# Gated mix of a recurrent memory attention and a GeGLU layer: one transpose excursion for k and q, o and v pieces in turn, fills in other gaps, scratch laid out anew

## The chip, the core and the metric

The kernel runs on one core of one Trainium2 chip. The metric is the device time of one execution in microseconds, as the median of several runs. TensorE (PE), VectorE (DVE), ScalarE (ACT), GpSimd (POOL) and SyncE (SP) run their own instruction streams in order and wait for each other on semaphores. Weights and activations are bf16, sums are held in PSUM as fp32.

## The reference, cut to what matters

```python
def A(x, mem0, Wq, Wk, Wv, Wo):            # x 1 x 2048 x 1024, 32 heads of 128, segments of 32 rows, memory of 8
    mem = mem0
    for s in range(64):
        h = concatenate([mem, x[:, 32*s:32*s+32]], axis=1)         # 40 rows
        q, k, v = (einsum('btd,dhe->bhte', h, W) for W in (Wq, Wk, Wv))
        scores = where(mask, einsum('bhqe,bhke->bhqk', q, k) * 128 ** -0.5, -1e9)
        o = einsum('bhqk,bhke->bhqe', softmax(scores), v)
        o = einsum('bhte,hed->btd', o, Wo)
        mem, out[s] = o[:, :8], o[:, 8:]
    return concatenate(out, axis=1)

def B(x, w_gate, w_up, w_down):            # 1024 x 3584, 1024 x 3584, 3584 x 1024
    return gelu(x @ w_gate) * (x @ w_up) @ w_down

g = sigmoid((x * gate_w).sum(-1, keepdims=True))
out = g * A(x) + (1 - g) * B(x)
```

A is a recurrence: each of its 64 steps needs the 8 memory rows that the step before left. The four weight matrices of A have 8 MB each, 32 MB together, and do not fit in SBUF; every step needs all of them.

## The kernel before

Three stages follow each other. A first stage transposes x, computes the gate and four of the 28 column blocks of the feed-forward layer, and fills SBUF with weights. Then come the 64 steps of the recurrence. Then the rest of the feed-forward layer and the mix.

**Steps and weights.** A step walks 64 positions in a fixed order (`walk`, line 327). A position is one piece of 512 KB of Wk, Wq, Wv or Wo: 128 rows by 16 heads, or two heads of Wo. `(m, r, i)` names piece `i` of matrix `m` in half `r` of the step; the half with `r = 0` works on 16 heads, `r = 1` on the other 16, and the next step begins with the half that was last. The walk is k and q of half 0 in turn, v of half 0, k and q of half 1, o of half 0, v of half 1, o of half 1. SBUF holds 52 pieces; 12 slots are shared by a pair of pieces, one of each half (`PAIRS`, line 318). When a shared slot's piece was used in half 0 (`spent`, line 385), SP fetches the other one (`fetch`, line 371, issue at line 378), so that 12 fetches of 512 KB are issued in a step. `proj` (line 784) computes a position: four matmuls in four 32-column tiles of TensorE (lines 796 and 779; 807 for o).

**Rows.** A segment's 32 rows and 8 memory rows make 40. The tile `hT` (line 525) has the transposed 24 first rows of the segment and the 8 memory rows. The last 8 rows (the rest) depend on no memory: for four segments at a time their q, k, v are computed ahead of the steps that need them, with the pieces that are in SBUF anyway. These are the fills (`fill`, line 822, eight positions each). Their results go to the scratch tensors `qk_scr` and `v_scr` in DRAM and come back one step ahead of use as `qkr` (line 534) and `vB` (line 538). Their attention outputs go to `o_scr`, come back as `oR`, and are multiplied with Wo by `wo` (line 837, also eight positions).

**One half of a step.** ScalarE evacuates k and q from PSUM into `tok` and `tok2` (line 677). TensorE turns each in an excursion to four 128 x 128 transposes (line 690); VectorE copies the results to `kT` and `qT` (line 680). `rest_k` (line 888, on POOL) adds the rest's k. `scores` (lines 711 to 718) does scores and softmax: a chain through VectorE and ScalarE, ten operations, whose results are `tA` (line 734) and `tB` (line 741). `attend` (line 752) needs `tA` and `vA`, `attend_tail` (line 762) `tB` and `vB`. ScalarE and VectorE evacuate the result to `oT`, and POOL copies the rest's part to `oRc` (line 773).

**Order.** `on(m, r, n, ...)` puts work ahead of position `n` of a part of the walk. In front of o of half 0 stand the eight positions of the first fill (`f1`), put between the evacuations, the two transposes, attend and its tail; `scores` of half 1 stands one position later. In front of o of half 1 stand the eight positions of the second fill (`f2`), six of them ahead of attend. At the step's end (from line 1018) ScalarE copies the output to `a_bf`, TensorE turns it in two transposes (line 1025), VectorE writes the 8 memory columns of the next `hT` (line 1027), and the next step starts. The output's store, `a_scr` from `a_bf` (line 1035), is issued from POOL within the next step. `pA`, which softmax writes, shares memory with `a_bf`.

The dependence tracker `_Prog` adds the semaphore waits. PSUM is tracked by bank, SBUF by 64-byte cells, and a DMA that has its own lane waits until the lane's last one has landed.

Of the kernel before, what the change touches and what calls it, by code (L numbers as in the profile page):

```python
# [195 lines left out]
def bass_gated_mix__memory_aug_recurrent_mem_tr__geglu_ffn__prompt_kernel(  # L196
# [20 lines left out]
    NR = 24  # L217
# [14 lines left out]
    with ExitStack() as es:  # L232
# [12 lines left out]
        v_scr = nc.dram_tensor("v_scr", [NSEG, NB, 16, 2, 128], BF16)  # L245
# [45 lines left out]
        qT = al("qT", [128, 4, 4, 32])  # L291
        cur[0] += 128
# [6 lines left out]
        vA = al("vA", [128, 4, 128], at=oT.off)  # L299
        tok2 = al("tok2", [128, 512], at=oT.off + 1024)  # L300
        tA = al("tA", [128, 8, 32], at=qT.off)
        tB = al("tB", [128, 8, 32], at=qT.off + 512)
        E8 = al("E8", [128, 8, LQ], at=qT.off + 512)
# [10 lines left out]
        oR2 = al("oR2", [128, RB, 16], at=odd0 + 1024)  # L314
        NSLOT = NLOW + (top - cur[0]) // PIECE


        PAIRS = {"k": (0, 2), "q": (0,), "v": (0, 1, 2, 3, 4, 6), "o": (0, 2, 4)}
# [8 lines left out]
        walk = both(0) + one("v", 0) + both(1) + one("o", 0) + one("v", 1) + one("o", 1)  # L327
# [112 lines left out]
        st0 = [al(f"st0{i}", [128, 512], at=slots[-1].off + 1024 * i) for i in range(4)]  # L440
        st1 = [stage] + [al(f"st1{i}", [128, 512], at=odd0 + 1024 * i) for i in range(2)]
# [81 lines left out]
        def load_h(s):  # L523
            t = hTs[s % 2]
            op("pool", lambda e: e.dma_start(t[:, :, :].rearrange("p k c -> p (k c)"), xq_scr[s // 4, :, s % 4, :]),
               rd=[("D", "xq", s // 4)], wr=[t.r()], lane=f"h{s % 2}")
# [5 lines left out]
        def load_qk(s, r):  # L532
            u = r ^ (s % 2)
            op("pool", lambda e: e.dma_start(qkr[:, r, :, :], qk_scr[:, s, 2 * u:2 * u + 2, :]),
               rd=[("D", "qk", s // 4, 2 * u), ("D", "qk", s // 4, 2 * u + 1)], wr=[qkr.r(256 * r, 256 * r + 256)], lane=f"qkr{r}")

        def load_v(s, us=slice(0, 2)):
            op("pool", lambda e: e.dma_start(vB[:, us, :].rearrange("p u c -> p (u c)"),
                                             v_scr[s][:, :, us, :].rearrange("i h u c -> h i (u c)")),
               rd=[("D", "v", s // 4, g, u) for g in range(4) for u in range(us.start, us.stop)], wr=[vB.r()], lane="vb")  # L540
# [13 lines left out]
        inits = [k for k in [at_step(p, 0) for p in range(24)] + [(m, 1, i) for m in "kqv" for i in range(8)]  # L554
# [129 lines left out]
        def evac(bank, t):  # L684
            act_copy(t[:, :], PB[bank][:, :], [BK(bank)], [t.r()])

        def trans4(e, t=tok, head=False):
            for j in range(4):
                to = PBV[TT][:, 0:512].rearrange("p (g j y) -> p j g y", g=4, j=4)[:, j] if head else PBV[TT][:, j * 128:(j + 1) * 128]
                ins = e.transpose(to, t[:, j * 128:(j + 1) * 128], ident[:, :])  # L690
            return ins

        def trans_pe(t):
            op("pe", lambda e: trans4(e, t), rd=[t.r(), ident.r()], wr=[BK(TT)])

        def trans(to, t):
            if t:
                trans_pe(t)
            i_ap = PBV[TT][:, 0:512].rearrange("p (j g c) -> p (j g) c", g=4, c=32)
            dve_copy(to[:, :, :, 0:32].rearrange("p j g c -> p (j g) c"), i_ap, [BK(TT)], [to.r()])  # L700
# [5 lines left out]
        def scores(r, mid=None):  # L706

            def f(e):
# [8 lines left out]
                for g in range(4):  # L717
                    ins = e.matmul(PB[SS][32 * g:32 * g + 32, 0:320].rearrange("p (a c) -> p a c", a=4)[:, :, LQ:80],
                                   lhsT=qkr[:, r, 0, 32 * g:32 * g + 32], rhs=kT[:, :, g, :],
                                   start=False, stop=True, skip_group_check=True)  # L720
                return ins
            op("pe", f, rd=[qT.r(), kT.r(), ident.r(), mS.r(), qkr.r(256 * r, 256 * r + 128)], wr=[BK(SS)])
            op("pool", lambda e: e.memset(pB[:, :].bitcast(FP32), 0.0), wr=[pB.r()])
            op("dve", lambda e: e.tensor_reduce(nm, sS, AX.X, ALU.max, negate=True), rd=[BK(SS)], wr=[st8.r(0, 8)])
            op("dve", lambda e: e.tensor_tensor(out=sS, in0=sS, in1=b8(nm, LQ), op=ALU.add), rd=[BK(SS), st8.r(0, 8)], wr=[BK(SS)])  # L725
            op("act", lambda e: e.activation(E8[:, :, :].rearrange("p a c -> p (a c)"), PB[SS][:, 0:320], ACTF.Exp, scale=scale),  # L726
               rd=[BK(SS)], wr=[E8.r()])
            if mid:
                mid()
# [14 lines left out]
        bo = (B0, B1, B2, SS)  # L744

        def attend(u):
# [11 lines left out]
        def attend_tail(u):  # L758
# [9 lines left out]
            for g in range(4):  # L768
                cp[("act", "dve")[g % 2]](oT[:, g, :, :].rearrange("p j c -> p (j c)"), PB[bo[g]][:, 0:n], [BK(bo[g])],
                                          [oT.r(g * n, (g + 1) * n)])  # L770
# [5 lines left out]
        bank_of = {("k", 0): B0, ("q", 0): B1, ("v", 0): B2, ("k", 1): B0, ("q", 1): F2, ("v", 1): B0}  # L776
# [36 lines left out]

        def fill(m, u, b, h=hR):
            ks = [(m, u, i) for i in range(8) if i not in PAIRS[m]] + [(m, u, i) for i in PAIRS[m]]
            out = []
            for n, k in enumerate(ks):
# [7 lines left out]
                out.append(lambda f=f, w=w: op("pe", f, rd=[h.r(), w.r()], wr=[BK(b)]))  # L825
            return out

        def wo(u, b, t=oR, ends=(True, True), at_end=False):
            out = []
            for i in range(8):  # L830
                w = (xo.get(("o", u, i)) if at_end else None) or slots[home["o", u, i]]

                def f(e, i=i, w=w):
                    for hh in range(2):
                        for g in range(4):
                            c = hh * 1024 + g * 256
                            ins = e.matmul(PB[b][32 * g:32 * g + 32, 0:256], lhsT=t[:, :, 2 * i + hh], rhs=w[:, c:c + 256],  # L837
                                           start=(ends[0] and i == 0 and hh == 0), stop=(ends[1] and i == 7 and hh == 1))
                    return ins
                out.append(lambda f=f, w=w: op("pe", f, rd=[t.r(), w.r()], wr=[BK(b)]))  # L840
# [8 lines left out]
        def fill_evac(m, u, b, st):  # L849
            t = st if m == "v" else tok  # L850
            act_copy(t[:, :], PB[b][:, :], [BK(b)], [t.r()])

        def fill_trans(m):
            op("pe", lambda e: trans4(e, tok, m == "q"), rd=[tok.r(), ident.r()], wr=[BK(TT)])

        def fill_put(st, how):
            cp[how](st[:, :].rearrange("p (i x c) -> p x i c", i=4, x=16), PBV[TT][:, 0:512].rearrange("p (x i c) -> p x i c", x=16, i=4),
                    [BK(TT)], [st.r()])

        def fill_store(m, u, G, st):  # L860
            if m == "v":
                for g in range(4):
                    op("pool", lambda e, g=g: e.dma_start(  # L863
                        v_scr[4 * G:4 * G + 4, :, 4 * g:4 * g + 4, u, :].rearrange("s i j c -> (s i) j c"),
                        st[32 * g:32 * g + 32, :].rearrange("p (j c) -> p j c", j=4)), rd=[st.r()], wr=[("D", "v", G, g, u)], lane=f"fv{g}")
            else:
                m4 = 2 * u + (0 if m == "q" else 1)
                op("pool", lambda e: e.dma_start(qk_scr[:, 4 * G:4 * G + 4, m4, :], st[:, :].rearrange("p (i y) -> p i y", i=4)),
                   rd=[st.r()], wr=[("D", "qk", G, m4)], lane="fq")

        def mm0(m, u, b, t, G=0, h=hR):
# [3 lines left out]
            if m == "v":  # L875
                fill_store(m, u, G, t)

        def tr0(m, u, t, b, G=0):
            op("pe", lambda e: trans4(e, t, m == "q"), rd=[t.r(), ident.r()], wr=[BK(TT)])
            fill_put(b, "dve")  # L880
            if G == 0:
                x = 256 * u + 128 * (m == "k")
# [297 lines left out]
```

## Time and profile before

| | us |
|---|---|
| median of 10 runs | 2207.38 |
| lowest, highest | 2202.39, 2215.53 |
| the profiled execution's own time | 2202.52 |
| its span, first to last instruction | 2200.8 |
| TensorE busy in it | 2031.7 |
| VectorE, ScalarE, POOL busy in it | 931.3, 606.8, 623.6 |

The granted TensorE clock was 0.993 over the span. In the profile, an instruction stands under the line of the kernel that made it, which for helpers is the helper's line, and under the names of its tiles (`out<-in`). "PEld" is the loading of weights into TensorE's array. A wait is put down to the instruction whose end released it; "issue" is time in which an engine waited for nothing that the profile shows.

### The profile page before, as it was taken

Reading aid. Unit: us, or ns where it says so; the run is one execution under the profiler, and the core shown is the slowest. Engines: PE = TensorE matmul, PEld = TensorE weight load, DVE = VectorE, ACT = ScalarE, POOL = GpSimd, SP = SyncE. Lnnn points to the kernel's source line nnn. Section 1 sums busy time; section 2 is a strip of 40 time slices with the busy share of each in tenths; the row PEclk is TensorE's granted clock in tenths of the full one; section 3 lists DMA queues with packets and bytes.
Section 4 is the critical chain, followed back from the end, with each engine's and each line's share of the span. In section 5 each row is a group of like instructions: output and inputs, shape, how many; then the busy total and the mean of one; then the engine's idle time right before and its main releaser. Section 6 shows DMA issues by size and latency. Waiting matters only on the chain.

```text
span 2200.8 us, 76740 instructions
## 1 busy us (share of the span) xinstructions
PE 2031.7 (92%) x37842; PEld 930.1 (42%) x32178; DVE 931.3 (42%) x2154; ACT 606.8 (28%) x1296; POOL 623.6 (28%) x1155
## 2 busy tenths in 40 slices
PE   7779999999999998999999999999888999999999
PEld 4334444444444444444444444444344424243343
DVE  6433443344344343433443444344344526254362
ACT  4322222323223232222323232232222303132130
POOL 7224334332433433343333334333321000000000
PEclk9989999999999999999999999999999999999999
DMA  9978888888888788878888888888789400001000
GB/s 365 374 275 273 296 309 278 297 305 290 275 300 314 272 296 285 299 272 275 319 281 280 302 304 285 284 313 295 266 310 369 146 21 29 30 29 30 23 27 20
DMA packets 202660, 528.84 MB, mean 240 GB/s; under 512 B 29592, under 2 KB 46616, under 8 KB 202336
## 3 DMA queue, kind: packets, MB, share of 16 engines
q1 hardware_dynamic: 171760, 466.69, 59.6%
q0 software_dynamic: 30432, 56.99, 8.3%
q8 instruction: 274, 4.49, 0.8%
q14 instruction: 50, 0.41, 0.1%
q10 hardware_dynamic: 144, 0.26, 0.0%
HBM read 490.16 MB, written 33.55 MB: 238 GB/s over the span
## 4 chain that ended last, share of the span: by engine, by line
PE 60%; DMA 25%; DVE 5%; POOL 5%; issue 3%; SPq 1%; ACT 1%; POOLq 0%; DVEq 0%
PE pb L462 15%; PE pb L796 12%; DMA sl<-in_A_Wv_dram 8%; PE pb L779 8%; PE pb L807 7%; DMA sl<-in_A_Wk_dram 6%; PE pb L822 5%; DMA a_scr<-a_bf 5%; PE pb L1135 4%; DMA sl<-in_A_Wo_dram 3%; PE pb L690 3%; DVE oT L680 2%; DMA xr_scr<-xr 2%; POOL v_scr L863 1%; PE pb L837 1%
## 5 line engine op out<-in xcount | busy, mean ns | idle before, releaser
L796 PE MATMUL pb<-sl,hT 128*32 128x512 bf16 x8192 | 667.8, 381 | 46.9 <-issue 22.5
L779 PE MATMUL pb<-sl,hT 128*32 128x512 bf16 x4096 | 398.5, 379 | 0.0
L796 PEld LDWEIGHTS pb<-sl,hT 128*32 128x32 bf16 x8192 | 211.7, 96 | 435.7 <-issue 272.6
L807 PE MATMUL pb<-sl,oT 128*32 128x256 bf16 x8192 | 276.9, 277 | 18.1 <-issue 9.9
L773 POOL COPY oRc<-oT 128x128 bf16<-128x128 bf16 x128 | 95.7, 748 | 646.0 <-DVE oT L680 646.0
L677 ACT ACTIVATE tok<-pb 128x512 bf16<-128x512 f32 x318 | 176.4, 596 | 345.8 <-PE pb L796 320.6
L807 PEld LDWEIGHTS pb<-sl,oT 128*32 128x32 bf16 x8192 | 202.6, 97 | 80.3 <-ACT oT L677 45.2
L822 PE MATMUL pb<-sl,hR 128*32 128x512 bf16 x3072 | 210.4, 385 | 0.0
L680 DVE COPY kT<-pb 128x512 bf16<-128x512 bf16 x128 | 53.2, 415 | 317.3 <-PE pb L690 296.0
L462 PE MATMUL pb<-xT,wg 128*128 128x512 bf16 x768 | 181.5, 379 | 3.9 <-DMA wg<-in_B_w_gate_dram 3.9
L462 PE MATMUL pb<-xT,wu 128*128 128x512 bf16 x768 | 181.4, 379 | 0.8 <-DMA wu<-in_B_w_up_dram 0.8
L680 DVE CAST oT<-pb 128x256 bf16<-128x256 f32 x256 | 96.7, 419 | 181.9 <-PE pb L762 181.9
L690 PE MATMUL pb<-ident,tok 128*128 128x128 bf16 x1272 | 126.7, 222 | 41.3 <-DVE kT L680 34.8
L1135 PE MATMUL pb<-wd,GT 128*32 128x512 bf16 x1568 | 152.2, 379 | 0.0
L779 PE MATMUL pb<-wd,GT 128*32 128x512 bf16 x1568 | 152.2, 379 | 0.0
L677 ACT ACTIVATE vA<-pb 128x512 bf16<-128x512 f32 x128 | 76.4, 597 | 269.3 <-PE pb L796 269.3
L450 ACT ACTIVATE s<-pb 128x512 f32<-128x512 f32 x112 | 66.9, 597 | 289.3 <-PE pb L462 289.3
L690 PEld LDWEIGHTS pb<-ident,tok 128*128 128x128 bf16 x1272 | 72.0, 98 | 150.9 <-DVE kT L680 83.1
L677 ACT ACTIVATE oT<-pb 128x256 bf16<-128x256 f32 x256 | 84.3, 381 | 183.6 <-PE pb L762 183.6
L451 DVE SCALAR_TENSOR_TENSOR tp<-s,pb 128x512 f32<-128x512 f32 x112 | 76.7, 685 | 123.4 <-ACT s L450 123.0
L726 ACT ACTIVATE E<-pb 128x320 bf16<-128x320 f32 x128 | 56.0, 437 | 219.3 <-DVE pb L725 219.3
L462 PEld LDWEIGHTS pb<-xT,wg 128*128 128x128 bf16 x768 | 74.8, 98 | 95.7 <-issue 6.3
(104 smaller groups left out, 2226.0 us busy)
## 6 DMA issues: line engine op xcount, KB each, us to landing
sl<-in_A_Wv_dram SPq DMA_DIRECT2D x394, 512.0 KB, 9.4
sl<-in_A_Wo_dram SPq DMA_DIRECT2D x205, 512.0 KB, 5.9
sl<-in_A_Wk_dram SPq DMA_DIRECT2D x142, 512.0 KB, 7.4
sl<-in_A_Wq_dram SPq DMA_DIRECT2D x79, 512.0 KB, 6.8
qkr<-qk_scr POOLq DMA_DIRECT2D x126, 64.0 KB, 2.4
qk_scr<-stg POOLq DMA_DIRECT2D x59, 128.0 KB, 6.9
wd<-in_B_w_down_dram SPq DMA_DIRECT2D x7, 1024.0 KB, 15.0
xq_scr<-xTp SPq DMA_DIRECT2D x4, 1024.0 KB, 17.1
```

The lines of the kernel that those rows point to most:

```text
L450: op("act", lambda e: e.activation(s1[:, :], hg, ACTF.Square, scale=SQ), rd=[BK(bg)], wr=[s1.r()])
L451: op("dve", lambda e: e.scalar_tensor_tensor(out=t[:, :], in0=s1[:, :], scalar=1.0, in1=hg, op0=ALU.add, op1=ALU.mult), rd=[BK(bg), s1.r() ...
L462: ins = e.matmul(PB[bk][:, 0:FB], lhsT=w[:, kc, cc:cc + 128], rhs=x[:, :, :, kc, :].rearrange("p t i c -> p (t i) c"), start=(kc == 0), st ...
L677: op("act", lambda e: e.activation(o, i, ACTF.Copy), rd=rd, wr=wr)
L680: op("dve", lambda e: e.tensor_copy(o, i), rd=rd, wr=wr)
L690: ins = e.transpose(to, t[:, j * 128:(j + 1) * 128], ident[:, :])
L773: op("pool", lambda e: e.tensor_copy(oRc[:, u, :, :].rearrange("p c (g j) -> p g j c", g=4), diag), rd=[oT.r()], wr=[oRc.r(128 * u, 128 * ...
L779: return e.add_instruction(mybir.InstMatmult(name=nc.get_next_instruction_name(), start_tensor_calc=start, stop_tensor_calc=stop, tile_siz ...
L796: ins = again(e, g, *at, one, end) if k[0] == "q" else e.matmul(*at, start=one, stop=end)
L807: ins = e.matmul(PB[XO][32 * g:32 * g + 32, 0:256], lhsT=oT[:, gp_, 2 * jj + hh, 0:32], rhs=w[:, c:c + 256], start=(r == 0 and one and hh ...
L822: ins = e.matmul(PB[b][32 * g:32 * g + 32, :], lhsT=h[:, k[2], :], rhs=w[:, g * 512:(g + 1) * 512], start=(n == 0), stop=(n == 7))
L1135: ins = again(e, q, *a, j == 0, j == NJ - 1) if hf else e.matmul(*a, start=(j == 0), stop=(j == NJ - 1))
```

## The change

- k and q of a half are evacuated by ScalarE and VectorE side by side, and turned in one excursion of eight transposes (`trans8`, `turn`); ScalarE copies kT and VectorE qT.
- o of half 0 and v of half 1 alternate in the walk. v has 5 shared slots instead of 6, o 4 instead of 3.
- Fills: of the first fill (`fa`) two positions stand ahead of the first attend, one behind its tail, five ahead of the second attend. Of the second (`fb`), four stand behind the second attend's tail, two ahead of the step end's transposes and two behind them. `wo` is part of `fb`. Q and K of a fill are turned together in the next step and stored in one DMA.
- `scores` of half 0 stands at position 1 of k half 1 (before: 2), that of half 1 at position 3 of o half 0 (before: 1).
- vA of half 1 is evacuated in halves, one by ScalarE and one by VectorE.
- At the step's end one `a_bf` half is copied by VectorE, and the two transposes become eight small matmuls in 32-column tiles.
- `v_scr` is laid out with the 16 heads of a half together: one store of 1 KB runs instead of four, and two loads of 256 B runs instead of one of 512 B. `qk_scr` is stored with k and q together.
- `qkr`, `hT` and `vB` are loaded from SP's ring instead of POOL's. `a_scr`'s store is issued at the first position of the next step.

```diff
-        v_scr = nc.dram_tensor("v_scr", [NSEG, NB, 16, 2, 128], BF16)
+        v_scr = nc.dram_tensor("v_scr", [NSEG, NB, 2, 16, 128], BF16)
...
-        vA = al("vA", [128, 4, 128], at=oT.off)
+        vAs = [al("vA0", [128, 4, 128], at=oT.off), al("vA1", [128, 4, 128], at=tok.off)]
+        qT = al("qT", [128, 4, 4, 32], at=stage.off)
...
-        PAIRS = {"k": (0, 2), "q": (0,), "v": (0, 1, 2, 3, 4, 6), "o": (0, 2, 4)}
+        PAIRS = {"k": (0, 2), "q": (0,), "v": (0, 1, 2, 3, 4), "o": (0, 1, 2, 3)}
...
-        walk = both(0) + one("v", 0) + both(1) + one("o", 0) + one("v", 1) + one("o", 1)
+        walk = both(0) + one("v", 0) + both(1) + [x for y in zip(one("o", 0), one("v", 1)) for x in y] + one("o", 1)
...
+        def load_qk(s):
+            op("sp", lambda e: e.dma_start(qkr[:, :, :, :].rearrange("p u m c -> p (u m c)"), qk_scr[:, s].rearrange("p m c -> p (m c)")),
+               rd=[("D", "qk", s // 4, u) for u in range(2)], wr=[qkr.r()], lane="qkr")
+
+        def load_v(s, us=(0, 1), eng="sp"):
+            for u in us:
+                op(eng, lambda e, u=u: e.dma_start(vB[:, u, :], v_scr[s][:, u].rearrange("i h c -> h i c")),
+                   rd=[("D", "v", s // 4, u)], wr=[vB.r(128 * u, 128 * u + 128)], lane=f"vb{eng}{u}")
...
+        def trans8(ka, qa, head=False):
+            def f(e):
+                trans4(e, ka)
+                return trans4(e, qa, head, 512)
+            op("pe", f, rd=[ka.r(), qa.r(), ident.r()], wr=[BK(TT)])
...
-        bo = (B0, B1, B2, SS)
+        bos = ((XO, SS, B2, F2), (B0, B1, B2, SS))
...
             on("v", 0, 0, lambda: evac(bank_of["k", 0], tok))
-            on("v", 0, 0, lambda: evac(bank_of["q", 0], tok2))
-            on("v", 0, 4, lambda: trans(kT, tok))
-            on("v", 0, 7, lambda: trans(qT, tok2))
-            on("k", 1, 0, lambda: evac(bank_of["v", 0], vA))
-            on("k", 1, 2, lambda: scores(0))
+            on("v", 0, 0, lambda: evac(bank_of["q", 0], stage, "dve"))
+
+            def turn():
+                trans8(tok, stage)
+                heads(kT, "act", 0)
+                heads(qT, "dve", 512)
+            on("v", 0, 4, turn)
+            on("k", 1, 0, lambda: evac(bank_of["v", 0], vAs[0]))
+            on("k", 1, 1, lambda: scores(ua))
+            on("k", 1, 1, softmax)
...
             on("o", 0, 0, lambda: evac(bank_of["k", 1], tok))
-            on("o", 0, 0, lambda: evac(bank_of["q", 1], tok2))
-            on("o", 0, 0, some(f1, 4))
-            on("o", 0, 0, lambda: trans(kT, tok))
-            on("o", 0, 0, some(f1, 2))
-            on("o", 0, 0, lambda: trans_pe(tok2))
-            on("o", 0, 0, lambda: attend(ua))
-            on("o", 0, 0, lambda: attend_tail(ua))
-            on("o", 0, 0, lambda: trans(qT, None))
-            on("o", 0, 0, some(f1))
...
+            on("o", 0, 0, lambda: evac(bank_of["q", 1], stage, "dve"))
+            on("o", 0, 0, some(fa, 2))
+            on("o", 0, 0, lambda: attend(ua, 0))
+            on("o", 0, 0, lambda: attend_tail(ua, 0))
+            on("o", 0, 0, some(fa, 1))
+            on("o", 0, 0, turn)
+            on("o", 0, 3, lambda: scores(ub))
+            on("o", 0, 3, softmax)
+
+            def halves(bank, t):
+                evac(bank, t, "act", 0, 256)
+                evac(bank, t, "dve", 256, 512)
+            on("o", 1, 0, lambda: halves(bank_of["v", 1], vAs[1]))
+            on("o", 1, 0, some(fa))
+            on("o", 1, 0, lambda: attend(ub, 1))
+            on("o", 1, 0, lambda: attend_tail(ub, 1))
+            if k2 and k2[0] == "v":
+                on("o", 1, 0, lambda: evac(F1, tok))
+                on("o", 1, 0, lambda: store_v(k2[1], G, tok))
+            on("o", 1, 0, some(fb, 4))
             if not last:
-                on("o", 1, 0, lambda: load_qk(s + 1, 0))
-                on("o", 1, 0, lambda: load_qk(s + 1, 1))
-                on("o", 1, 0, lambda: load_v(s + 1))
+                on("o", 1, 0, lambda: load_qk(s + 1))
                 if s + 2 < NSEG:
                     on("o", 1, 0, lambda: load_h(s + 2))
+                on("o", 1, 0, lambda: load_v(s + 1))
...
-            for t in range(2):
+            for t, eng in enumerate(("act", "dve")):
                 cs = slice(128 * t, 128 * t + 128)
-                act_copy(a_bf[:, cs], PB[XO][:, cs], [BK(XO)], [a_bf.r(cs.start, cs.stop)])
...
+                cp[eng](a_bf[:, cs], PB[XO][:, cs], [BK(XO)], [a_bf.r(cs.start, cs.stop)])
+            run(fb, 2)
             if not last:
...
+                for t, bk, eng in ((0, B2, "dve"), (1, SS, "act")):
+                    def f(e, t=t, bk=bk):
+                        for g in range(4):
+                            c = 128 * t + 32 * g
+                            ins = e.matmul(PB[bk][32 * g:32 * g + 32, 0:32], lhsT=a_bf[:, c:c + 32],
+                                           rhs=ident[:, :].rearrange("p (g c) -> p g c", g=4)[:, :, NR:32], start=True, stop=True)
+                        return ins
...
+            run(fb)
+
+            def a_store(s=s):
...
+            pend = [(0, [a_store])]
+            if k1:
+                pend.append((0, [lambda: evac(F1, tok2), lambda: evac(F2, tok, "dve")]))
+
+                def fills_in(u=k1[1], G=G):
+                    trans8(tok2, tok, True)
+                    fill_put(fqk[:, :, 1, :], fqk.r(), "act")
+                    fill_put(fqk[:, :, 0, :], fqk.r(), "dve", 512)
+                    store_qk(u, G, fqk)
+                pend.append((3, [fills_in]))
```

## The prediction

> **What bounds the kernel now.** I read the page first, then busy time by stretch, the order of time of TensorE and of VectorE through one step, the waits, and the DMA issues.
>
> ```profile
> 0.00:122.00 122.00, 92.15 (x752) 44.20 (x724) 61.46 (x94) 42.15 (x76) 54.54 (x65) 0.94 1.00 373
> 122.00:1661.00 1539.00, 1409.50 (x32158) 677.39 (x28086) 628.94 (x1707) 446.51 (x1028) 548.40 (x1054) 0.99 0.84 291
> 1661.00:2200.00 539.00, 530.06 (x4940) 208.47 (x3372) 240.89 (x354) 118.17 (x193) 20.70 (x37) 1.00 0.19 67
> ...
> 1041.00:1059.00 18.00, 16.88 (x400) 8.26 (x344) 8.78 (x23) 4.90 (x10) 6.84 (x14) 1.00 1.01 353
> 1059.00:1064.50 5.50, 5.01 (x129) 2.53 (x112) 1.10 (x4) 1.59 (x5) 3.91 (x8) 1.00 0.41 120
> ```
>
> Columns: stretch, length, busy PE, PEld, DVE, ACT, POOL, clock, DMA share, GB/s. The 64 steps of the recurrence take 1539 of 2200.8 us; 62 intervals between their ends (hT copies, L1027) run from 144.5 to 1637.5, 24.08 us each. The feed-forward stage hardly meets the diff. In a step DMA is full for 18 us (1.01) and nearly idle for 5.5: two chains of almost equal length, the engines' and the weight stream's.
>
> ```profile
> 1018.97 1.04 PE L796 MATMUL pb<-sl,hT 128*32 128x512 bf16 x16
> 1019.93 0.40 PE L690 MATMUL pb<-ident,tok 128*128 128x128 bf16 x4
> 1020.26 0.83 PE L796 MATMUL pb<-sl,hT 128*32 128x512 bf16 x12
> ...
> 1028.43 0.40 PE L807 MATMUL pb<-sl,oT 128*32 128x256 bf16 x8
> 1029.13 0.32 PE L711 MATMUL pb<-mS,ident 128*32 128x320 bf16 x4 [0.30 <-DVE qT L680]
> ...
> 1036.43 1.93 PE L807 MATMUL pb<-sl,oT 128*32 128x256 bf16 x64
> 1038.74 0.40 PE L1025 MATMUL pb<-ident,a_bf 128*128 128x128 bf16 x2 [0.38 <-ACT a_bf L677]
> 1039.24 0.40 PE L796 MATMUL pb<-sl,hT 128*32 128x512 bf16 x4
> ```
>
> ```profile
> 1029.67 0.49 DVE L724 TENSOR_REDUCE st<-pb 128x8 f32<-128x320 f32 x1 [0.59 <-PE pb L718]
> 1032.42 0.45 DVE L734 STREAM_TRANSPOSE tA<-pA 128x256 bf16<-128x256 bf16 x1
> 1033.01 0.45 DVE L741 STREAM_TRANSPOSE tB<-pB 128x256 bf16<-128x256 bf16 x1
> ```
>
> The first fence is TensorE in order of time (start, length, what, count, and in brackets idle time before it and what ended it), the second VectorE in the same step. Four things to read. A position of four matmuls costs 0.216 us (16 matmuls, 0.86), one of Wo about the same. An excursion to four 128x128 transposes costs 0.43: 0.10 late, then 0.33. From the last Wo matmul's turn (1038.11) to the next step's first (1039.24), 1.13 us hold no projection. And the softmax chain: call its first scores matmul S (1029.13); tA is done at S+3.74, tB at S+4.33.
>
> ```profile
> DVE pA L732 <- DMA a_scr<-a_bf: 27.7, 27, 2.8
> PE pb L690 <- DVE kT L680: 34.8, 30, 11.1
> DVE kT L680 <- POOL kT L888: 20.6, 2, 15.7
> POOL qk_scr L868 <- DMA qk_scr<-st: 16.4, 3, 6.8
> ```
>
> ```profile
> sl<-in_A_Wv_dram SPq DMA_DIRECT2D x394, 512.0 KB, 9.4
> sl<-in_A_Wo_dram SPq DMA_DIRECT2D x205, 512.0 KB, 5.9
> qkr<-qk_scr POOLq DMA_DIRECT2D x126, 64.0 KB, 2.4
> ```
>
> The waits (total us, times, longest), then the DMA issues (times, KB each, median us from issue to landing). pA shares memory with a_bf, so softmax waits until a_bf is stored; that store is issued on POOL behind the V stores.
>
> **Part by part, us per step, plus is gained.**
> - Step end: two fills' positions (0.44) now run behind the last Wo, then the transposes, two more behind them. a_bf is ready 0.62 after 1038.11 (matmul 0.25, ACT 0.28 and two hops), so 0.18 is waited, 0.15 spent on the eight small matmuls that replace two transposes (bounds: 0.10, in which sixteen 40-column L715 start, and 0.24, the two transposes' own); the hT copy (0.175) hides under the second pair. Visible 0.33 of 1.13: +0.80. Fills themselves are moved, not added. Without that cover, 0.
> - k and q in one excursion: 0.10 + 0.33 + 4 x 0.06 = 0.67 for 0.86, twice: +0.39. The fills' excursion at the third position of the next step costs 0.67 in 28 of 64 steps, where before K's 0.43 was paid and Q's hid at step end: -0.10.
> - The wait of scores on qT (1028.65 to 1029.13) goes: six positions now lie between: +0.48.
> - The store of a_bf is first on POOL at the next step's start, past the V stores (2.2 us of issues), which become one. Gaps before L690 that hang on this sum to 26 us: +0.41. What is late next there is tB.
> - First attend: scores to attend was 5.1 us of PE work, now 0.31 + 14 x 0.216 + 2 x 0.216 = 3.76. tA just comes, the tail waits for tB: 4.37 against 3.99. Then stage: its cast on DVE is queued behind tB and takes 0.62 (two 256-column casts, 0.38 and 0.38, less one start of 0.15, since hT's 32 columns take 0.175), so the transposes wait 0.14 more: -0.52. Behind this on PE stands the alternating block, behind stage on DVE two oT copies and qT; qT is ready at S+6.2, scores come at S+6.9, so nothing more is late. Bounds: -0.38 if PE arrives later, -0.6 with 0.69 for the cast (as a 512-column tensor op).
> - Second attend: before, 4.7 us lay between; now five o and five v positions, five fills: 0.31 + 2.16 + 1.08 + 0.10 = 3.65. vA is now half DVE's, queued behind tB: 4.33 + 0.38 + 0.04 = 4.75. All of attend waits, and behind it on PE the Q or Wo fills and the second half of Wo: -1.10. Bounds: -0.6 (a PE stall falls inside the window) and -1.5 (slower hops).
> - Weights: 12 fetches as before (k 2, q 1, v 5 for 6, o 4 for 3). In the step from 1039.24 they landed at 4.9, 7.5, 9.4; 10.8, 12.9, 14.2, 15.5, 16.8, 18.0; 19.5, 20.8, 22.3. PE waits between matmul starts on weights sum to 31.5 us (k 15.7, v 11.6, o 4.2), to "issue" 38.7. One V fewer ahead and the small loads out of the way bring the last V to about 16.2; its use is at 16.0 to 16.5, and up to 1.1 of lateness falls into the second attend's wait: +0.18. K: half its waits, +0.12. The last o lands near 21.5, wanted at 20.6 to 21.4: -0.2 to -0.5, -0.25 taken. Issue stalls inside the two attends' windows are absorbed: 0.3 of 0.6, of that half, +0.07. Together +0.12; bounds -0.5 and +0.4.
> - Small loads on SP's ring: qkr, hT, vB (256 KB) stand behind the four o fetches. They wait only for PE work that precedes the next fetch in program order, so no fetch is held (vB's load waits for the second attend's tail, and behind it on SP stand the next step's K fetches, due 4 us later); they land about 23, qkr is wanted 2.6 into the next step. POOL loses four issues (0.55 each). Taken 0, bounds -0.2 and +0.1.
> - tok now is V's fill buffer: its store must land before the next k evacuation, 6.5 us after issue. V stores took 6.6 at the median, but when DMA is emptier 4.3 to 4.9. 0 taken, bound -0.2.
>
> By rows this is 0.80 + 0.39 - 0.10 + 0.48 + 0.41 - 0.52 - 1.10 + 0.12 = +0.48 a step, x 62 = 30 us.
>
> Step 0 apart: PE stands 11.1 us before its second transposes, since kT's tail copy on POOL is behind four K/Q stores, each waiting for the last to land (5.4 to 6.8). Now there are two. The copy comes at about 107 instead of 114.6, and a V store of one issue saves a little later: 8 us, bounds 4 and 12.
>
> The Trainium skill, page DMA: Bandwidth & Descriptors, section Specifications, speaks against one edit: transfers under 512 B cost a read-modify-write, and vB's load goes from 512 B runs to 256 B. No run here shows it; if 64 KB (0.2 us of 16 engines at 353 GB/s) doubled, an estimate by that page is -0.2 a step where the stream decides, and the sum +0.28. Packets in the trace from 250 to 1600 us took 209 ns for 4 KB on POOL's queue, runs of all lengths mixed, and 183 on SP's: no sign of a doubling, so I keep 0 in the sum.
>
> Sum: 38 us from the profiled 2202.5 (span 2200.8 and 1.7 around it) gives 2164.5. The median of the ten runs, 2207.4, lies 4.9 higher; at that level 2169.
>
> **Rivals.**
> 1. The weight stream decides, slower. From the last o's landing L, 0.22 + 1.21 us remain, so a step is at least L + 1.43. At 21.5 that is 22.9 and does not bind; at the old 22.3 it is 23.7. It costs time from L = 22.8 (24.21, step 0's 8 us counted). For it: DMA full from 2 to 20 us, K/Q stores of 256 KB in one burst, short runs. Against: fewer bytes ahead of it. At L = 23.2: 24.63, +34 - 8 = +26: 2233.
> 2. The second attend's wait does not show (tB and vA arrive as PE does): +1.10 more, held by the stream at 22.9: 1.18 x 62 + 8 = 81: 2126. Against: DVE is in order.
> 3. The two waits are larger (0.4 in sum): +0.08 a step, 13 us with step 0: 2194. If step 0's stores still block, it is 2202, hardly told from no change.
>
> **How the numbers follow.** Forecast 0.58, rival 1 0.16, rival 2 0.11, rival 3 0.15. A measurement of this kernel tells about 0.2%, 4.4 us. Faster: 0.58 + 0.11 + 0.10 = 0.79; same 0.05; slower 0.16. The unknown terms, taken together, reach from -0.4 to +0.4 a step, which is 2144 to 2194 for the forecast alone. Eight in ten take in rivals 2 and 3 and rival 1's weak end: 2122 to 2212.
>
> **What would show it.** Steps of 23.6 us; a gap of about 1.1 before the second attend, released by DVE's vA; one of 0.4 before the first attend's tail; eight L690-like transposes together; no pA wait on a_scr; 0.4 instead of 1.1 at step end; step 0's stall under 5 us. Wrong if Wo waits pass 30 us in sum (rival 1), or no PE gap stands at the second attend (rival 2).

## The result, and the profile after

The changed kernel takes 2228.4 us (median of 15 runs, 2216.1 to 2231.1) against 2209.0 for the kernel before (52 runs on the same chips): ratio 1.008, interval [1.0065, 1.0095]. It is slower by 0.8%; the forecast was 2169, 38 us faster. The sign that the prediction gave for its rival 1, "Wo waits pass 30 us in sum", is there.

Busy time by stretch of the profiled execution after (span 2222.0 us, own time 2224.0); the columns are those of the prediction's first fence, the last two rows one step:

```profile
0.00:122.00 122.00, 95.09 (x780) 44.84 (x748) 61.88 (x95) 43.12 (x78) 51.87 (x61) 0.96 0.97 361
122.00:1661.00 1539.00, 1370.33 (x32160) 675.82 (x28124) 704.01 (x1775) 431.18 (x984) 355.50 (x673) 0.99 0.84 287
1661.00:2222.00 561.00, 547.32 (x5288) 217.18 (x3684) 250.65 (x379) 123.40 (x205) 23.58 (x42) 0.99 0.22 78
1095.00:1113.00 18.00, 16.73 (x375) 7.82 (x308) 10.17 (x25) 5.58 (x12) 2.79 (x7) 1.00 0.94 325
1113.00:1119.30 6.30, 4.63 (x132) 2.83 (x128) 1.41 (x5) 1.15 (x5) 1.40 (x3) 1.00 0.55 188
```

Over the whole execution POOL lost 193 us of work (623.6 to 430.9) and TensorE 19 (2031.7 to 2012.7), while VectorE gained 85 (931.3 to 1016.5). (The second row shows 39 less for TensorE, but the recurrence of after runs past 1661.) The steps grew: the first hT copy of the recurrence comes at 144.2 in both, the last at 1637.2 before and 1656.0 after, that is 24.08 and 24.38 us a step. All but some 2 of the 21 us between the two profiles lie there. The waits of TensorE's matmuls (total us, times, longest):

```profile
PE pb L811 <- DMA sl<-in_A_Wo_dram: 53.1, 71, 2.5
PE pb L800 <- DMA sl<-in_A_Wv_dram: 31.1, 56, 2.0
PE pb L811 <- issue: 27.7, 26, 2.7
PE pb L754 <- DVE vA L679: 20.5, 34, 1.8
PE pb L766 <- DVE tB L742: 14.0, 52, 3.2
...
PE pb L830 <- ACT stv L676: 6.3, 1, 6.3
PE pb L800 <- DMA sl<-in_A_Wk_dram: 5.0, 8, 1.5
```

Counted as the prediction counted them, by the gaps between matmul starts, the waits for weights went from 31.5 us to about 121: Wo from 4 to 67, Wv from 12 to 47, Wk from 16 to 7. The waits for kT (34.8 before) and for a_scr's store are gone. Two ends of a step of after, TensorE in order of time:

```profile
1093.03 0.40 PE L811 MATMUL pb<-sl,oT 128*32 128x256 bf16 x8 [0.75 <-DMA sl<-in_A_Wo_dram]
1093.26 0.60 PE L830 MATMUL pb<-sl,hR 128*32 128x512 bf16 x8
1093.82 0.53 PE L1027 MATMUL pb<-ident,a_bf 128*32 128x32 bf16 x8
1094.18 0.60 PE L830 MATMUL pb<-sl,hR 128*32 128x512 bf16 x8
1094.61 0.39 PE L800 MATMUL pb<-sl,hT 128*32 128x512 bf16 x4
...
1112.13 1.25 PE L830 MATMUL pb<-sl,hR 128*32 128x512 bf16 x20
1113.31 0.29 PE L754 MATMUL pb<-tA,vA 32*128 32x64 bf16 x16
1113.44 0.24 PE L766 MATMUL pb<-tB,vB 32*128 32x160 bf16 x4
1113.61 1.05 PE L830 MATMUL pb<-sl,hR 128*32 128x512 bf16 x16
1114.48 1.27 PE L811 MATMUL pb<-sl,oT 128*32 128x256 bf16 x40
1117.30 0.84 PE L811 MATMUL pb<-sl,oT 128*32 128x256 bf16 x24 [1.55 <-issue]
1117.95 0.62 PE L830 MATMUL pb<-sl,hR 128*32 128x512 bf16 x8
1118.51 0.53 PE L1027 MATMUL pb<-ident,a_bf 128*32 128x32 bf16 x8
1118.87 0.60 PE L830 MATMUL pb<-sl,hR 128*32 128x512 bf16 x8
1119.30 0.39 PE L800 MATMUL pb<-sl,hT 128*32 128x512 bf16 x4
```

The first end is the common one: the last Wo piece landed at 1092.99, and the last position (8 matmuls) starts with it, after a wait of 0.75 us. From there to the next step (1094.61) only the step end is left: 1.35 us from the last Wo matmul's turn (1093.26), 0.86 of them fills, so 0.49 without them.

The second end shows another wait. Its two L811 rows are the half's eight positions of Wo, five and three, and the step's four Wo fetches, for the last four positions, landed at 1113.16, 1114.46, 1116.01 and 1117.28. The wait of 1.55 us stands ahead of the sixth position, whose piece had landed at 1114.46. The row says "issue", and it is not a wait for weights, though it ends with the last landing: a packet of instructions had arrived at 1115.68 (see the section on the hardware). The DMA issues of after:

```profile
sl<-in_A_Wv_dram SPq DMA_DIRECT2D x331, 512.0 KB, 8.5
sl<-in_A_Wo_dram SPq DMA_DIRECT2D x268, 512.0 KB, 7.0
...
qkr<-qk_scr SPq DMA_DIRECT2D x63, 128.0 KB, 7.9
```

63 fetches moved from Wv to Wo; a Wo fetch now takes 7.0 us to land for 5.9.

For what follows a step is cut at its first Wk fetch (issued 0.45 us after the step's first projection in both kernels): the **window** runs from there to the last landing of the step's 12 fetches, and the rest to the next such fetch. Means of 50 steps: before 21.78 + 2.36 us, after 22.09 + 2.32. The two add up to the step by definition; what the experiments can tell is whether the step follows the window.

### The profile page after: what moved, and what is told of

It reads as the page before. It is cut to its first block, busy times and chain, and to the rows that moved or that the text cites. A ratio compares the mean times of both kernels' runs of the same rounds, so it can differ in the third digit from the quotient of the medians.

```text
span 2222.0 us, 77508 instructions
## 1 busy us (share of the span) xinstructions
PE 2012.7 (91%) x38220; PEld 937.8 (42%) x32556; DVE 1016.5 (46%) x2248; ACT 597.7 (27%) x1266; POOL 430.9 (19%) x776
## 4 chain that ended last, share of the span: by engine, by line
PE 59%; DMA 25%; DVE 10%; issue 2%; ACT 2%; POOL 1%; SPq 0%; POOLq 0%; DVEq 0%; ACTq 0%
DMA sl<-in_A_Wo_dram 19%; PE pb L462 16%; PE pb L800 13%; PE pb L783 9%; PE pb L811 5%; PE pb L690 4%; PE pb L1153 4%; PE pb L830 2%; DMA sl<-in_A_Wk_dram 2%; DMA sl<-in_A_Wv_dram 2%; PE pb L849 1%; DVE pb L726 1%; DVE st L725 1%; DVE st L731 1%; DVE tB L742 1%
## 5 line engine op out<-in xcount | busy, mean ns | idle before, releaser
L800 PE MATMUL pb<-sl,hT 128*32 128x512 bf16 x8192 | 731.0, 384 | 38.8 <-DMA sl<-in_A_Wv_dram 31.1
L811 PE MATMUL pb<-sl,oT 128*32 128x256 bf16 x8192 | 353.8, 276 | 84.2 <-DMA sl<-in_A_Wo_dram 53.1
L783 PE MATMUL pb<-sl,hT 128*32 128x512 bf16 x4096 | 404.6, 385 | 0.0
L811 PEld LDWEIGHTS pb<-sl,oT 128*32 128x32 bf16 x8192 | 207.5, 97 | 174.8 <-DMA sl<-in_A_Wo_dram 59.2
L830 PE MATMUL pb<-sl,hR 128*32 128x512 bf16 x3072 | 218.7, 385 | 12.2 <-ACT stv L676 6.3
L676 ACT ACTIVATE tok<-pb 128x512 bf16<-128x512 f32 x192 | 114.7, 598 | 269.3 <-PE pb L800 255.2
L679 DVE CAST stg<-pb 128x512 bf16<-128x512 f32 x128 | 86.2, 673 | 167.8 <-PE pb L783 167.7
L679 DVE CAST a_bf<-pb 128x128 bf16<-128x128 f32 x64 | 18.6, 291 | 249.1 <-ACT a_bf L676 249.1
L679 DVE COPY qT<-pb 128x512 bf16<-128x512 bf16 x128 | 54.3, 425 | 132.5 <-ACT kT L676 132.5
L462 PEld LDWEIGHTS pb<-xT,wu 128*128 128x128 bf16 x768 | 75.5, 98 | 91.9 <-issue 2.2
L830 PEld LDWEIGHTS pb<-sl,hR 128*32 128x32 bf16 x3072 | 78.9, 97 | 83.8 <-issue 19.9
```

Of the source, the lines that this page charges most:

```text
L462: ins = e.matmul(PB[bk][:, 0:FB], lhsT=w[:, kc, cc:cc + 128], rhs=x[:, :, :, kc, :].rearrange("p t i c -> p (t i) c"), start=(kc == 0), st ...
L676: op("act", lambda e: e.activation(o, i, ACTF.Copy), rd=rd, wr=wr)
L679: op("dve", lambda e: e.tensor_copy(o, i), rd=rd, wr=wr)
L783: return e.add_instruction(mybir.InstMatmult(name=nc.get_next_instruction_name(), start_tensor_calc=start, stop_tensor_calc=stop, tile_siz ...
L800: ins = again(e, g, *at, one, end) if k[0] == "q" else e.matmul(*at, start=one, stop=end)
L811: ins = e.matmul(PB[XO][32 * g:32 * g + 32, 0:256], lhsT=oT[:, gp_, 2 * jj + hh, 0:32], rhs=w[:, c:c + 256], start=(r == 0 and one and hh ...
```

## The experiments

Theory S: the stream of weights sets the step, as window plus about 2.3 us, and what the engines save turns into waits for weights. Rival D: the stream has slack, and the two attend waits on VectorE, larger than priced, eat the savings. Ratios are to the kernel before on the same chip, with 95% intervals.

**Half the bytes (a_half, b_half).** Every refetch of a shared slot moves the first 256 KB only, so the outputs are those of stale weights; in the kernel after (a_half) and in the one before (b_half).

```diff
+            cut = done[n] > 0 and paired(k)
...
+                return e.dma_start(t[:, 0:1024], src(k)[:, 0:1024])
```

> The changed kernel with every refetch of a shared slot cut to its first half (256 KB of 512): from its second turn on a shared slot holds the other piece's second half, so the output is not the reference's; instructions and waits are the same. Theory S (the weight stream sets the step, and what TensorE saved became waiting for weights): without that bound the step falls from 24.4 to TensorE's own 22.4 to 22.9 us, about 2130 us in all, weight waits near nothing, and the gaps at the two attends come into view. Rival D (the two attends' waits on VectorE made it slower, and the weight waits are what was left over): the step stays at 23.8 or more, 2190 us or more, and it is not faster than the kernel before with the same cut.

> The kernel before with every refetch of a shared slot cut to its first half (256 KB of 512), output not the reference's for that reason. Theory S: it loses only its 0.5 us a step of weight waits, 24.1 to 23.6, about 2178 us, so it is 1.5 to 2.5% slower than the changed kernel with the same cut. Rival D: equal to or faster than the changed kernel with the same cut.

Measured: 2092.3 us, 0.9461 [0.9441, 0.9481], and 2103.4, 0.9511 [0.9491, 0.953]. No gap for weights is left in either trace, nor any of the "issue" gaps in the projections. Waits of a_half (its lines stand 8 lower than those of after):

```profile
PE pb L762 <- DVE vA L687: 66.1, 64, 2.0
PE pb L774 <- DVE tB L750: 18.8, 64, 5.3
```

By matmul starts the gap before the second attend is 1.25 us in 59 steps, the tail's 0.40 in 64. The attends do wait as forecast, and without the stream's bound a step takes 22.42 us after and 22.49 before: the change gains 0.07. All else, 106 us before and 136 after, is what the bytes of the stream add. Both theories missed on b_half: S expected 2178 and a lead of 1.5 to 2.5% for a_half, which leads by 0.5%, and D expected no lead, and 2190 or more for a_half. The kernel before loses more to the stream than its 31.5 us of waits for weights: "issue", half of kT's wait (34.8 to 18.4 us) and a_scr's store go with the bytes too.

**One fetch less (a_11, b_11).** One shared pair of Wo is never refetched (its second half is stale), 11 fetches a step for 12.

```diff
-            if done[n] < len(uses[n]) and uses[n][done[n]] != k:
+            if done[n] < len(uses[n]) and uses[n][done[n]] != k and n != home["o", 0, 3]:
```

> The changed kernel with 11 fetches a step for 12: the slot of the last shared Wo piece is never refetched, so that piece is the same one in both halves and the output is not the reference's. Theory S: the last landing comes one fetch (1.4 us) earlier and the step follows it until TensorE's own path takes over, 24.4 to 23.0 to 23.3, about 2150 us. Rival D: below 0.5 us a step, 2200 us or more.

> The kernel before with 11 fetches a step for 12, the slot of its last shared Wo piece never refetched (output not the reference's). Theory S: TensorE's own path takes over after 0.5 us a step, so 23.6, about 2178 us: less gained than by the changed kernel from the same cut. Rival D: both gain the same.

Measured: 2156.8 us, 0.9748 [0.9727, 0.9769], a step of 23.39, and 2200.2, 0.9944 [0.9921, 0.9968]. After, one fetch less is worth 72 us, 1.0 us in each step, of the 1.48 that a fetch takes of the DMA (17.8 us for 12, below); before, 12 us, where waits for Wk (27.6 us by matmul starts), for a_scr's store and "issue" stay. In the kernel after this is S. In the kernel before S expected 2178: there the last Wo ends few of the steps (the section on the prediction counts them).

**The second attend's wait (a_act).** vA of half 1 is evacuated by ScalarE alone, past VectorE's queue.

```diff
-                evac(bank, t, "act", 0, 256)
-                evac(bank, t, "dve", 256, 512)
+                evac(bank, t)
```

> The changed kernel with vA of half 1 evacuated by ScalarE alone, so that the second attend no longer waits for a copy queued behind tB on VectorE. Theory S: that wait lies beside the wait for the last Wo piece, so the time stays within 6 us of the changed kernel's 2228. Rival D: 0.4 us a step is gained at the second attend, 2203.

Measured: 2227.9 us, 1.0087 [1.0056, 1.0118]. TensorE's waits in it:

```profile
PE pb L811 <- DMA sl<-in_A_Wo_dram: 55.5, 77, 2.5
PE pb L811 <- issue: 32.1, 28, 2.4
PE pb L800 <- DMA sl<-in_A_Wv_dram: 30.6, 51, 1.7
PE pb L766 <- DVE tB L742: 11.3, 54, 0.3
```

The wait of 20.5 us on vA is gone from the list, Wo and "issue" have 6.8 more, and the time has not moved. D falls.

**Where the small loads are issued (a_pool, b_sp).** The kernel after with qkr, hT and vB on POOL again; the kernel before with them on SP's ring (the same lines, the other way).

```diff
-        def load_h(s, eng="sp"):
+        def load_h(s, eng="pool"):
...
```

> The changed kernel with the small loads (qkr, hT, vB) issued from POOL again, their shapes as changed. Theory S with the small loads as the cause of the longer chain (they stand in SP's ring, 512 and 256 byte runs): the time from the first K trigger to the last landing falls from 22.1 to 21.8 or less, 0.3 us a step, 2209 us. If the place of the loads is not the cause: within 5 us of the changed kernel, 2223 to 2233.

> The kernel before with its small loads (qkr, hT, vB, in their old shapes) issued on SP's ring and nothing else changed. If their place is what costs (theory S, small loads): slower by 10 to 15 us, 2219 to 2224, with the first weight landings later or the last one 0.2 later. If the ring does not matter: 2204 to 2214.

Measured: a_pool 2215.2 us, 1.0019 [0.9997, 1.0041]; b_sp 2186.8, 0.9891 [0.9869, 0.9912]. So 0.6% of the 0.8% goes with this edit, which alone gains 1.1%: a miss in both directions. In b_sp the window is 21.45 us (before 21.78) and kT's wait is halved (34.8 to 18.0 us). It is the fastest of the kernels that fetch all their weights.

**Slots and order (a_pairs, b_pairs, a_walk, a_walkpool).** a_pairs has the old shared slots in the kernel after, a_walk the old slots and the old order of o and v, a_walkpool also the loads on POOL; b_pairs has the new slots in the kernel before.

```diff
-        PAIRS = {"k": (0, 2), "q": (0,), "v": (0, 1, 2, 3, 4), "o": (0, 1, 2, 3)}
+        PAIRS = {"k": (0, 2), "q": (0,), "v": (0, 1, 2, 3, 4, 6), "o": (0, 2, 4)}
```

> The changed kernel with the shared slots of before (six of v, three of o). Theory S with Wo's pieces as the cause (2 KB runs, landing 1.45 us apart against 1.35): the chain shortens by 0.1 us a step, 2222 us; a v piece more is wanted earlier, up to 0.3 us a step of new v waits against that, 2222 to 2240. If neither matters: 2228.

> The kernel before with the shared slots of the changed one (five of v, four of o), nothing else changed. Theory S with Wo's pieces as the cause of the longer chain: 0.1 us a step slower, 2215; with the fourth o landing last and wanted at the end: up to 0.3, 2228. If the shared slots do not matter: 2209.

> The changed kernel with the walk and the shared slots of before (o of half 0, then v of half 1; six of v, three of o). Theory S: six v pieces are wanted 1 to 2 us later than in turn with o, so the waits for v (0.7 us a step in the changed kernel) mostly go; the chain of 12 landings stays. 0.2 to 0.4 us a step gained, 2203 to 2216. If the order of the walk does not matter: 2221, as with the slots alone.

> The same with the small loads on POOL as well. If both effects add up: 2190 to 2203, as fast as or faster than the kernel before. If the loads' place is only worth something where v waits bind: 2203 to 2216.

Measured: a_pairs 2221.3 us, 1.007 [1.0043, 1.0096]; a_walk 2217.1, 1.004 [1.002, 1.0061]; a_walkpool 2224.4, 1.0074 [1.0048, 1.0101]; b_pairs 2267.0, 1.0273 [1.0241, 1.0304]. With the old slots the weight waits of the kernel after are on Wv in place of Wo: by TensorE's wait rows in the recurrence, 110.5 us in a_pairs and 75.2 in a_walk, where after has 53.1 on Wo and 29.3 on Wv. They move rather than go. a_walkpool, expected at 2216 at most, and b_pairs, at 2228 at most, came out slower. b_pairs is no clean test, as half 1 there also waits 19.1 us for oT (4.9 before).

**The same in the kernel before, cleaner (b_alt, b_altsp).** Before with the new slots, the alternating order, and oT of half 1 evacuated in the order of its use; b_altsp also with the loads on SP.

```diff
+        PAIRS = {"k": (0, 2), "q": (0,), "v": (0, 1, 2, 3, 4), "o": (0, 1, 2, 3)}
...
+        walk = both(0) + one("v", 0) + both(1) + [x for y in zip(one("o", 0), one("v", 1)) for x in y] + one("o", 1)
...
+            on("o", 1, 0, lambda: attend_tail(ub, (2, 3, 0, 1)))
```

> The kernel before with the changed kernel's order of o and v pieces and its shared slots (v 5, o 4), and nothing else of the change; the small loads stay on POOL. Theory W (order and slots are what lengthens the window of fetches): first trigger to last landing 22.0 to 22.3 us against 21.8, most of the weight waits on Wo and Wv, 2213 to 2225 us. Theory R (the other parts lengthen it: excursions, fills, layouts): 21.8 us and 2203 to 2212.

> The same with qkr, hT and vB on SP's ring. In the kernel before that move was worth -1.1%, in the changed kernel +0.6%. Theory W (the order and slots turn its sign): 2220 to 2235, at or above the one with the loads on POOL. Theory R (the sign is turned by another part): 1% below the one with the loads on POOL, 2180 to 2200.

Measured: 2268.7 us, 1.0275 [1.0239, 1.0312], and 2272.4, 1.0287 [1.0257, 1.0317]: dearer than either theory said, and with no effect of the loads. Stretches of 1 us of a step of b_alt, whose first Wk fetch was issued at 1044.87 (the DMA share is the last but one column):

```profile
1058.00:1059.00 1.00, 1.00 (x32) 0.60 (x28) 0.93 (x3) 0.93 (x3) 0.11 (x1) 1.00 0.79 307
1059.00:1060.00 1.00, 0.91 (x44) 0.65 (x44) 0.40 (x2) 0.05 (x1) 0.84 (x2) 1.00 0.15 53
1060.00:1061.00 1.00, 0.78 (x22) 0.39 (x15) 0.75 (x2) 0.19 (x1) 0.00 (x0) 1.00 0.60 184
1061.00:1062.00 1.00, 0.87 (x25) 0.85 (x28) 0.68 (x2) 0.25 (x1) 0.00 (x0) 1.00 1.03 395
```

The stream runs dry in mid-step: 1.46 us are lost here. The packets of the five V fetches are all but through when the first Wo fetch is issued, at 1058.96, behind the eight fills that the old order puts ahead of o; its own packets begin 1.0 us later. In means of 50 steps, the first Wo fetch is issued 13.6 us into the window with 2.3 older ones still to land; in the kernel before at 13.6 with 3.4 (six V fetches bridge it), in the kernel after at 12.3 with 3.2. b_alt's window is 23.2 us. The clock took its part: from the first hT copy to the last it was 0.5 for 89 us in b_alt and 78 in b_pairs, against 10 in the kernel before, which is up to 40 of the 81 us between the profiles of b_alt and before. In the changed kernel, with the fills in their new place, the new slots are about level with the old (a_pairs against the kernel after, 1.007 and 1.008); they are not what makes the change slower.

**The store of a_bf (b_store).** In the kernel before, a_scr's store is issued ahead of the V stores; both, and the stores of K and Q, are issued at the next step's first position.

```diff
-            on("k", 0, 4, some(pend))
+            on("k", 0, 0, some(pend))
...
-                if k2[0] == "v":
-                    on("o", 1, 3, lambda: fill_store(*k2, G, stage))
...
-                if k2 and k2[0] == "q":
+                if k2:
```

> The kernel before with the store of a_bf moved ahead of the V stores on POOL (and to the next step's first position), nothing else. The prediction's term: softmax's wait on that store (27.7 us of VectorE, 26 us of TensorE) goes and 26 us are gained, 2183. Theory S: the stream takes most of it back as waits for weights, 5 to 12 us gained, 2197 to 2204, while the wait on the store is gone from the profile.

Measured: 2195.2 us, 0.9949 [0.9928, 0.9971], -13 us by the medians where the prediction's term gives 25. The wait of pA on that store, 27.7 us before, is gone; the waits on Wv have grown (6.8 us before):

```profile
PE pb L796 <- DMA sl<-in_A_Wv_dram: 18.3, 23, 1.6
```

**Single gains together (d1, d2).** d1 is b_sp with b_store's edit, d2 is d1 with the changed kernel's step end, without fills in it.

```diff
-            for t in range(2):
+            for t, eng in enumerate(("act", "dve")):
...
-                    op("pe", lambda e, t=t, bk=bk: e.transpose(PBV[bk][:, 0:128], a_bf[:, 128 * t:128 * t + 128], ident[:, :]),
...
+                            ins = e.matmul(PB[bk][32 * g:32 * g + 32, 0:32], lhsT=a_bf[:, c:c + 32],
+                                           rhs=ident[:, :].rearrange("p (g c) -> p g c", g=4)[:, :, NR:32], start=True, stop=True)
...
```

> The kernel before with two single edits together that were each faster alone: small loads on SP's ring (-22 us) and a_bf's store ahead of the V stores (-11 to -14). If each takes another wait away: 2170 to 2178. If the store's gain is part of the weight stream's window that the loads already shortened: 2184 to 2190. A slower one than 2195 speaks against the theory that the stream's window decides.

> The last one with the changed kernel's step end (a_bf copied by ScalarE and VectorE, eight small matmuls, two engines copying hT), no fills there. The prediction priced the step end as a whole at 0.8 us a step; without the fills there it is the shorter copy and matmuls alone, some 0.2 us a step on the engines' path. Where the stream decides it gives 0 to 5 us, where the engines decide 12: 2158 to 2190 by the level of the one without it.

Measured: d1 2191.7 us, 0.9931 [0.9903, 0.9958]; d2 2195.1, 0.9953 [0.9935, 0.9972]. The gains do not add: both are a little above b_sp, and above what was expected of them. d2's step end brings nothing that this measurement tells. In the profiled executions (2202.9, 2186.9 and 2186.8 us) d1's window is 21.57 us, d2's 21.34, b_sp's 21.45, so these executions are ordered as their windows; the medians are not (d1 is below d2). That the window alone sets the level is not shown.

## Why the prediction was wrong

**The step that failed is "Weights": "The last o lands near 21.5", and behind it "at 21.5 that is 22.9 and does not bind".** Counted from the step's first projection as there, the last landing is at 22.23 before (21.78 + 0.45) and 22.54 after. The prediction reasoned that one V fewer ahead lets the rest land earlier. But there were 12 fetches before and after, and their packets took about the same time in either order. (The prediction also called DMA "nearly idle" in the last 5.5 us of a step, where its row has a share of 0.41.) The window's time by DMA records, in us of all 16 engines (idle is what is left of the window):

| | weights | small, SP | small, POOL | instructions | idle | window |
|---|---|---|---|---|---|---|
| before | 17.58 | 0.11 | 1.69 | 0.23 | 2.17 | 21.78 |
| after | 17.81 | 1.00 | 1.05 | 0.23 | 1.99 | 22.09 |
| b_sp | 17.63 | 0.76 | 0.85 | 0.23 | 1.98 | 21.45 |
| b_pairs | 18.31 | 0.11 | 1.54 | 0.23 | 3.26 | 23.46 |

After, the weights cost 0.23 more (with the old slots in the same kernel, a_pairs, 17.57, so it goes with o in place of v), the small transfers 0.25 more, and 0.18 less is idle: +0.30, the longer window.

**The bound behind it was too small as well.** "From the last o's landing L, 0.22 + 1.21 us remain", 1.43 in all. The least that remains is seen in steps whose last Wo position starts with the landing. In after these are 46 of 62 steps, with 1.64 us on average (1.62 in the first end shown). Before they are 19 of 62, with 1.33. In the other steps of before TensorE was behind the stream:

```profile
1060.16 1.93 PE L807 MATMUL pb<-sl,oT 128*32 128x256 bf16 x64
1062.48 0.40 PE L1025 MATMUL pb<-ident,a_bf 128*128 128x128 bf16 x2 [0.39 <-ACT a_bf L677]
1062.97 0.40 PE L796 MATMUL pb<-sl,hT 128*32 128x512 bf16 x4
```

The last landing, at 1061.59, comes in the midst of the 64 Wo matmuls, and nothing waits for it. So the prediction was right that the stream of before had slack: 22.23 + 1.33 = 23.56 against a step of 24.1. After the change the same sum is 22.54 + 1.64 = 24.18, more than the old step. Half of that rise of 0.62 is the later landing. The other half is the four fill positions, which now stand behind the last Wo: four steps of after end without fills, and in three of them 1.33 us remain, as before (the fourth, 1.56, lies in a stretch of half clock). The step-end term, +0.80, counted these fills as cover, but behind a landing that all wait for they lengthen the step. No run puts them back ahead of the last Wo. The 24.38 measured are 0.2 above the sum; 14 steps have an "issue" wait about the last landing, with 2.36 us behind it in place of 1.64.

Rival 1 named the mechanism. Its own condition, a landing at 22.8 or later, was not met; its time was reached because more remains behind the landing, and because step 0 gave nothing.

**The engines' terms were right in size.** Without pA and weights they sum to -0.05 a step; a_half against b_half gives +0.07. So the forecast gain of 0.48 was all in pA (0.41) and weights (0.12), two waits for DMA. The second attend waits 1.25 where nothing else binds (predicted 1.10), the first one's tail 0.40 (0.4), the step end 0.49 without fills (0.33), eight transposes from the first's start to the next matmul 0.55. The sum added them up for a step that, after the change, mostly ends with the stream. The weights term, +0.12, was about -1.4 by its own count (31.5 to 121 us). The pA term, +0.41, was half given back as Wv waits (b_store).

**Small loads on SP's ring, "Taken 0, bounds -0.2 and +0.1"**: +0.35 a step alone (21.5 us), -0.21 inside the change (13 us). Both are beyond the bounds; b_sp's smaller window fits its sign, and no run accounts for the other.

**Step 0, "8 us": nothing.** The wait of 11.1 us and kT's late copy are gone (it runs at 109.7 for 114.6), but a fill waits 6.3 us for stv at 86.9, and fills at 111 to 121 for the first weights, 2.3 at the longest. The recurrence starts at 144.2 in both. Where weights do not hold it the term is there in part: 139.0 in a_half, 144.1 in b_half.

**Part of the same 19 us went through the clock and the last steps.** In the recurrence the granted clock was 0.5 for 10 us before and 34 after; at half speed that is up to 12 us more. Without the steps that hold such windows, and so without the waits ahead of them, the mean step is 24.03 before and 24.18 after. The last four steps, which have no fills to cover the second attend, are 7 us longer in sum; three of them hold such windows too.

Still open: why the loads on SP's ring gain in the kernel before, do nothing with the new slots there (b_altsp against b_alt), gain 0.3% in the changed kernel with the old order and slots (a_walk against a_walkpool, intervals that overlap) and lose 0.6% in it as it is. A shorter window goes with the gain in b_sp alone: a_pool's, 22.03, is hardly shorter than after's.

## What to carry to other kernels

Where two chains are close, cut the bytes of one of them in half in thought, and if possible on the chip, before any saving on the other is summed. From the trace of before, add to the last landing of the step's fetches the least that must stand behind it; what is missing to the step is all that the engines can gain before the stream binds. Work that is moved to the step's end as cover lengthens this bound if it stands behind the last landing. A wait that ends with a landing need not be for it: see which piece the position needs. Reordering fetches in the changed kernel moved the window's end by some 0.3 us (21.75 in a_walk, 22.09 in after), but a freed buffer that comes too late lets the queue run dry (b_alt, b_pairs), so slots and the work ahead of their last use are changed together.

## What the runs showed of the hardware

**The clock falls after short stalls.** Two stretches of after, then TensorE in the second of them:

```profile
1262.00:1265.70 3.70, 1.04 (x40) 0.79 (x36) 0.00 (x0) 0.00 (x0) 1.52 (x3) 1.00 0.50 141
1265.70:1269.10 3.40, 3.40 (x60) 1.41 (x44) 0.91 (x3) 0.47 (x2) 1.53 (x3) 0.50 0.17 33
```

```profile
1265.07 0.62 PE L811 MATMUL pb<-sl,oT 128*32 128x256 bf16 x16 [2.66 <-issue]
...
1267.27 0.64 PE L800 MATMUL pb<-sl,hT 128*32 128x512 bf16 x4
1267.69 0.64 PE L783 MATMUL pb<-sl,hT 128*32 128x512 bf16 x4
```

One wait of 2.66 us, and for the next 3.4 us the granted clock is 0.50 and a position takes 0.43 us for 0.216: where the clock falls, the wait costs up to 1.7 us again. Sums of shorter waits did it too (0.99 and 0.73 us ahead of 289.5), while single ones of 2.51 and 2.27 us did not. In the 3.4 us ahead of the falls at 289.5, 801.5, 948.2 and 1265.7 TensorE was busy for 0.74 to 1.59 us. The Trainium skill, page TensorE: Matmul & The Clock Gate, part 1, puts the fall behind at least one idle window of about 3.4 us; here less was enough.

**"issue" follows the fetching of instructions.** By the wait rows of the recurrence TensorE waited 32.6 us before and 31.3 after for nothing that the profile names; with the refetches halved 0.9 us are left in b_half and none in a_half. Instructions come by DMA too, in packets of 16 KB that take 1.05 us each before and 1.04 after, some four in a step. Of these waits 51 are longer than 0.5 us (27 before, 24 after), and every one ends 1.25 to 1.65 us behind the end of such a packet, as the one at 1117.30 does. That fits a TensorE that has run out of instructions while the weights fill the DMA engines. The trace does not show which engine a packet is for or when it was asked for; in a_half the packets take as long (1.08 us).

**Short runs cost little.** From 250 to 1600 us of after, packets of 256 B on SP's queue took 18.3 ns, of 512 B 27.9, of 4 KB 187. For vB's 64 KB that is 0.29 us of 16 engines for 0.22, +0.07 a step. The Trainium skill, page DMA: Bandwidth & Descriptors, section Specifications, would have the short ones pay a read-modify-write; a doubling does not show.
